# Moving ScalarE casts, batch sums and operand pieces to other work units in a fused attention and two-layer kernel

## The chip, the core and the metric

The kernel runs on one core of a Trainium2 chip. The metric is the time of one execution in microseconds (us), as the device reports it; lower is better. The engines are called as in the profile: PE is TensorE (PEld its weight loads), DVE is VectorE, ACT is ScalarE, POOL is GpSimd, SP is SyncE, which here issues nearly all DMAs.

## The reference

For 4 batches and 8 heads (sequence 768, head dimension 64) queries and keys are hashed by the signs of six projections. A score counts only where query and key fall into the same bucket; the rest get -1e9. The softmax of the scores times V is the attention output. The heads of a token side by side are a row of x, 3072 rows of 512. Then h = x @ w_in (512 x 2048), g is a piecewise function of h (0 below -1, h above 1, (h + 1)^2 / 4 between), and the result is g @ w_out (2048 x 512). All of it is float32.

## The kernel before, in words

**Split numbers.** A float32 product on PE is made of three matmuls of rounded parts: hi x hi, hi x lo, lo x hi. For every operand somebody makes the rounded part (a cast, on ACT in most places: "hi") and the rest (a subtraction, on DVE or POOL: "lo"). Much of the work beside the matmuls is of this kind, and all lo parts have the one line L39.

**Attention.** `attention` (line 125) walks over 384 units: 32 heads of 12 units, two query halves of six key tiles each. A unit, numbered head.unit from here on (16.5 is unit 5 of head 16), consists of: two score matmuls (L391, L392) into one of four score banks; two exponentials on ACT (L400 rounded, L405 exact); the rest `pl` on DVE, or for key tiles 0 and 3 on POOL; three output matmuls (L424, L426, L428) for the unit four before, in the tile order 1, 2, 0, 4, 5, 3. In the units 3 and 9 of every head ACT also copies a finished output half out of its bank (L434). Two heads ahead of use the row maxima are found: two matmuls (L323) into the only `smax` bank at the end of every even unit, and a reduction on DVE (L327) in the next. The last of them is clamped on POOL (L357, L359), turned on PE (L368) and put away.

**Tasks.** Everything else hangs on units through a list `tasks`: `at(g, fn)` runs `fn` at the end of unit g, in the order in which it was entered. An engine executes its instructions in program order, so the place of a task decides what stands behind it. The tasks that the change and the prediction speak of:

- `weights(p)`, lines 1084 to 1108, for p = 0 to 7, begins at head 3 + 3p. It loads two blocks of w_in, restores their words (ACT line L70 in unit 9, the "scaled word"; DVE L76, L79, L83 in units 9 to 2) and makes seven blocks: the hi and lo of three, the differences (`diff`, POOL), and then the hi (`shis`, ACT, L1073) and lo (`slos`, POOL) of four sums.
- Batch sums: `sums_add` (DVE L703, L704) and `sums_inv` (DVE reciprocal L708 and a DMA), lines 1127 to 1131, in head 11, 19 and 27.
- `FirstX` (line 725): operand pieces of the first batch for the second part. `load` brings data (three DMAs on SP), `fill` is one ACT instruction, `norm` two on POOL; a piece is then made by `sums` (a sum or difference of two parts), `hi` (ACT, L754) and `lo` (POOL). fx[0] and fx[1] work on 192 columns, with sums on POOL; fx[2] works on 384 columns in the heads 28 to 31, with sums on DVE (L751).
- In even heads POOL casts and splits the next q and k (`cast_h`, `low_h`, from unit 0 on), and PE uses them for the hash bits in the units 5 and 7 (L221).

**Second part.** `ffn` (line 762) walks over 224 steps k, seven to a pair of blocks of w_in (s = k % 7). Each step has six matmuls for h (L959) in one of two banks and five or six for y (L855). Step s = 0 copies its sum on ACT (`cm`, L964), and the matmuls of s = 2 go on in the same bank. Step 6 ends with two activations on ACT. `x_plan` (lines 896 to 904) makes the operand of the next batch; lines 1195 to 1209 make the hi and lo of w_out, with the cast (L96) on ACT.

Of the kernel before, what the change touches and what calls it, by code (L numbers as in the profile page):

```python
# [671 lines left out]
NBLK = 7  # L672
# [48 lines left out]
def cut(t, n):  # L721
    return t[:, n * CH:(n + 1) * CH]
# [39 lines left out]
def ffn(ctx, tc, woh, wol, xm, areas, ring, wst, wc, out, prep, post):  # L762
# [3 lines left out]
    nc = tc.nc  # L766
# [40 lines left out]
    def act_in(src):  # L807
        t = gp.tile([P, CH], F32, name="t")
        z = gp.tile([P, CH], F32, name="z", bufs=3)
        nc.scalar.activation(out=t, in_=src, func=AF.Relu, scale=0.5, bias=mh)  # L810
        nc.scalar.activation(out=z, in_=t, func=AF.Relu, scale=1.0, bias=m1)  # L811
        return [None, None, z, t]
# [81 lines left out]
    def x_plan(b, cc, raw, er, norm, made):  # L894

        at(raw, x_raw, b, cc)
        for k, n in enumerate(norm):
            after(n, x_norm, b, cc, k)
            at(er[k], x_er, b, cc, k)
        for o, n in zip((0, 1, 3, 2, 4, 5, 6), made):  # L900
            if o in SUMS:
                after(n, x_sum, o)
            after(n, x_hi, b, cc, o)
            after(n + 1, x_lo, b, cc, o)
# [8 lines left out]
    for b in range(1, B):  # L913
        n = (b - 1) * 56
        if b == 2:
            x_plan(b, 0, n + 8, range(n + 8, n + 12), [n + m for m in (15, 16, 18, 22)],
                   [n + m for m in (23, 25, 26, 28, 30, 31, 32)])
            x_plan(b, 1, n + 34, range(n + 26, n + 34, 2), [n + m for m in (37, 39, 43, 44)],
                   [n + m for m in (46, 47, 48, 50, 51, 53, 54)])
        else:  # L920
            x_plan(b, 0, n + 9, range(n + 9, n + 21, 3), [n + m for m in (16, 19, 23, 26)],
                   [n + m for m in (28, 30, 31, 32, 34, 35, 37)])
            x_plan(b, 1, n + 39, range(n + 30, n + 38, 2), [n + m for m in (43, 44, 46, 48)],
                   range(n + 49, n + 56))
    at(57, lambda: xm.sums_load(*(t[:, 0:NF] for t in pc[4:6]), B - 1))
# [17 lines left out]
    for k in range(NK):  # L943
        b, i, s = k // 56, k % 56 // NBLK, k % NBLK
        blk, o, bank = PRODUCTS[s]
# [8 lines left out]
        n = 0  # L954
# [25 lines left out]
        if src is not None:  # L980
            g = act_in(src)
# [23 lines left out]
def lsh_attn_ffn(ctx: ExitStack, tc: tile.TileContext, qk, v, pj, cv, w_in, w_out, out):  # L1005
    nc = tc.nc
# [12 lines left out]
    xm = XMaker(nc, x_d, s_d, er_d)  # L1019

    def flat(t):
        return t.rearrange("p a b s -> p (a b s)")
# [17 lines left out]
    def at(g, fn, *a):  # L1040
        tasks[g].append((fn, a))

    def conv(g, steps, offs):
        for fn, n in zip(steps, offs):
            at(g + n, fn)
# [6 lines left out]
    def wi_steps(f, dst):  # L1052
        return ws.word_steps(win_v[:, :, f * P:(f + 1) * P, :], (P, NCT, P, 2), lambda: dst, word)[1]
# [3 lines left out]
    def wo_staged(h, f):  # L1057
        stage = xdp.tile([P, DM], F32, name=f"wd{f}")
        first, *late[f] = ws.staged(wout_v[f], (P, DM, 2), stage, word)
        conv(h * NU, first, (0, 9, 10, 11, 14, 16))  # L1060
# [23 lines left out]
    def weights(p):  # L1084
        h0, r = 3 + 3 * p, rw[p % 2]
        f0, f1 = r[:, 0::3], r[:, 1:3]
        conv(h0 * NU, wi_steps(2 * p, f0), (0, 9, 10, 11, 14 - (p == 0)))
        conv((h0 + 1) * NU, wi_steps(2 * p + 1, f1), (0, 9, 10, 11, 14))
        wo_staged(h0 + 2, p)
        if p % 2 == 0:  # L1090
            his, los, subs = (26, 29), (28, 30), (32, 33, 34)
            puts, shis, slos = (34, 58), (50, 51), (52, 54)
        else:
            his, los, subs = (17, 36), (20, 40), (41, 42, 42)
            puts, shis, slos = (44, 57), (44, 45), (45, 47)
        g = h0 * NU
        for n, (d, x) in enumerate(((hp[:, 0:2], f0), (hp[:, 2:3], r[:, 2:3]))):
            at(g + his[n], hi, d, x)
            at(g + los[n], lo, d, x)
        for n, (d, x, y) in enumerate(((r[:, 0:2], r[:, 1:3], r[:, 0:2]), (r[:, 2], r[:, 2], r[:, 0]),  # L1100
                                       (r[:, 3], r[:, 2], r[:, 3]))):
            at(g + subs[n], diff, d, x, y)
        for n in range(2):
            sl = slice(2 * n, 2 * n + 2)
            at(g + shis[n], hi, hs[:, sl], r[:, sl])
            at(g + slos[n], lo, hs[:, sl], r[:, sl])
        at(g + puts[0], put, p, 0, hp)
        at(g + puts[1], put, p, 3, hs)

    for p in range(NFT // 2):  # L1110
        weights(p)
# [3 lines left out]
    g0 = (NH - 4) * NU  # L1115
# [11 lines left out]
    for b in range(B - 1):  # L1127
        g = (b + 1) * H * NU + LAG + 4
        at(g, lambda b=b: xm.sums_load(*(attn["small"].tile([P, NF], F32, name=n, bufs=1) for n in ("sm", "em")), b))
        at(g + 30, xm.sums_add)  # L1130
        at(g + 30, xm.sums_inv, b)

    def rows(t):
        return [t[:, 2 * k * CH:(2 * k + 2) * CH].bitcast(F32).rearrange("p (t n) -> p t n", t=2) for k in range(4)]

    def four(t, n):
        return [cut(t, n + k).bitcast(F32) for k in range(4)]
# [3 lines left out]
    def piece_wide(k):  # L1141
        if not wide:
# [3 lines left out]
    fx = [FirstX(nc, xm, cc, sl, pc, raw, er, lambda o, t, cc=cc: cut(wbig, 2 * NBLK * cc + 2 * o + t),  # L1146
                 lambda: attn["sv"])
          for cc, sl, pc, raw, er in ((0, slice(0, CH // 2), lambda k: xq[:, k], four(wbig, 8), rows(wbig)),
                                      (0, slice(CH // 2, CH), lambda k: xq[:, k], four(wbig, 8), rows(wbig)),
                                      (1, slice(0, CH), piece_wide, four(flat(T1[i0]), 0), rows(flat(T2[i0]))))]  # L1150
# [5 lines left out]
    def unit(h, n):  # L1156
        return h * NU + n

    def piece(x, o, g, eng_hi, eng):
        if o in FirstX.SUMS:  # L1160
            at(g, x.sums, o, eng)
        at(g + (o in FirstX.SUMS and eng_hi is not eng), x.hi, o, eng_hi)
        at(g + (eng_hi is not eng) * (1 + (o in FirstX.SUMS)), x.lo, o, eng)

    at(unit(10, 8), load_sv)
    for k, (h, n) in enumerate(((11, 6), (11, 9), (13, 6), (13, 9))):
        at(unit(h, n), fx[0].load, k)
    for n, gs in enumerate((((13, 1, 5), (13, 3, 7), (15, 1, 5), (15, 3, 10)),
                            ((23, 1, 5), (23, 3, 7), (25, 1, 4), (25, 3, 5)))):
        for k, (h, a, m) in enumerate(gs):  # L1170
            at(unit(h, a), fx[n].fill, k)
            at(unit(h, m), fx[n].norm, k)
    for n, plan in enumerate((((2, 17, 5), (0, 17, 7), (1, 17, 10), (3, 19, 3), (5, 19, 6), (4, 19, 9), (6, 21, 9)),
                              ((2, 25, 6), (0, 25, 8), (1, 25, 10), (3, 27, 9), (5, 28, 0), (4, 28, 3), (6, 28, 7)))):
        for o, h, m in plan:
            piece(fx[n], o, unit(h, m), nc.scalar, nc.gpsimd)
    for k, (n, a, m) in enumerate(((1, 9, 11), (2, 12, 13), (7, 16, 17), (9, 19, 20))):
# [2 lines left out]
        at(g0 + m, fx[2].norm, k)  # L1180
    for o, n in ((0, 22), (1, 24), (2, 26), (3, 28), (5, 31), (4, 34), (6, 37)):
        if o in FirstX.SUMS:
            at(g0 + n, fx[2].sums, o, nc.vector)
        at(g0 + n + 1, fx[2].hi, o, nc.scalar)
        at(g0 + n + 2, fx[2].lo, o, nc.gpsimd)
    for k in range(5):
# [9 lines left out]
    for f, n in sorted(starts.items(), key=lambda x: x[1]):  # L1196
        if f in late:
            get, back = late[f]
            prep[n].append((get, ()))
            n_cast, n_low = n + 3, n + 4  # L1200
        else:
            back, (s0, *steps) = ws.word_steps(wout_v[f], (P, DM, 2), ws.square)
            prep[n - 5].append((s0, ()))
            for fn, m in zip(steps, (0, 0, 1, 3)):
                post[n + m].append((fn, ()))
            n_cast, n_low = n + 4, n + 6
        cast, low = ws.split(back, woh[f], wol[f], nc.scalar, nc.vector)
        post[n_cast].append((cast, ()))
        post[n_low].append((low, ()))
    areas = [flat(t) for t in (T2[i0], T2[i1], T1[i0])], wbig  # L1210
    ffn(ctx, tc, woh, wol, xm, areas, ring, wst, wc, out, prep, post)


# [48 lines left out]
```

## Time and profile before

| what | us |
|---|---|
| median of three runs | 976.39 (975.54 to 976.45) |
| the profiled execution | 976.73 |
| its span, first to last instruction | 975.0 |
| PE busy | 955.5 (98% of the span) |
| DVE, ACT, POOL busy | 741.2, 686.8, 383.3 |

The page's slices show PE at nine tenths or more throughout, its granted clock at full speed throughout (1.00 is 2.4 GHz), and POOL at work until 465 us only: there the attention part ends. Matmuls are pipelined, and their modelled ends overlap the next start; so waits of PE are best read from starts.

### The profile page before, as it was taken

Reading aid. Unit: us, or ns where it says so; the run is one execution under the profiler, and the core shown is the slowest. Engines: PE = TensorE matmul, PEld = TensorE weight load, DVE = VectorE, ACT = ScalarE, POOL = GpSimd, SP = SyncE. Lnnn points to the kernel's source line nnn. Section 1 sums busy time; section 2 is a strip of 40 time slices with the busy share of each in tenths; the row PEclk is TensorE's granted clock in tenths of the full one; section 3 lists DMA queues with packets and bytes.
Section 4 is the critical chain, followed back from the end, with each engine's and each line's share of the span. In section 5 each row is a group of like instructions: output and inputs, shape, how many; then the busy total and the mean of one; then the engine's idle time right before and its main releaser. Section 6 shows DMA issues by size and latency. Waiting matters only on the chain.

```text
span 975.0 us, 15653 instructions
## 1 busy us (share of the span) xinstructions
PE 955.5 (98%) x5002; PEld 879.8 (90%) x5002; DVE 741.2 (76%) x1299; ACT 686.8 (70%) x1522; POOL 383.3 (39%) x512
## 2 busy tenths in 40 slices
PE   8999999999999999999999999999999999999998
PEld 7899999999899999998888898889998889888886
DVE  8778888888888888887688886677765777655554
ACT  7789999899899999999556656454564455644444
POOL 8767888778889888897000000000000000000000
PEclk9999999999999999999999999999999999999999
DMA  6775666878776677582895846765457464454431
GB/s 163 190 181 144 186 192 192 253 225 258 204 225 171 193 238 215 150 274 71 247 249 187 232 115 192 206 166 168 120 166 221 122 212 122 141 162 119 117 100 65
DMA packets 84633, 174.37 MB, mean 179 GB/s; under 512 B 13460, under 2 KB 35080, under 8 KB 83528
## 3 DMA queue, kind: packets, MB, share of 16 engines
q1 hardware_dynamic: 84282, 173.34, 61.9%
q8 instruction: 40, 0.66, 0.3%
q14 instruction: 41, 0.34, 0.1%
q10 hardware_dynamic: 270, 0.04, 0.0%
HBM read 116.35 MB, written 30.46 MB: 151 GB/s over the span
## 4 chain that ended last, share of the span: by engine, by line
PE 66%; ACT 9%; DVE 9%; DMA 5%; POOL 5%; issue 3%; SPq 1%; ACTq 0%; DVEq 0%; POOLq 0%
PE y L855 24%; PE h L959 21%; PE smax L323 4%; PE s L391 3%; PE s L392 3%; PE o L428 3%; PE o L424 3%; PE o L426 3%; ACT ph L400 2%; DVE nm L327 2%; DMA wraw<-in_w_out_dram 2%; PE o L221 2%; ACT s L405 2%; DVE pl L39 1%; POOL pl L39 1%
## 5 line engine op out<-in xcount | busy, mean ns | idle before, releaser
L400 ACT ACTIVATE ph<-s 128x384 fp32r<-128x384 f32 x380 | 190.4, 501 | 22.8 <-PE s L392 17.6
L327 DVE TENSOR_REDUCE nm<-smax 128x1 f32<-128x768 f32 x189 | 180.0, 952 | 23.1 <-PE smax L323 22.4
L39 DVE TENSOR_TENSOR pl<-s,ph 128x384 fp32r<-128x384 f32 x256 | 139.1, 551 | 34.0 <-ACT s L405 29.8
L816 DVE SCALAR_TENSOR_TENSOR t<-t 128x384 f32<-128x384 f32 x128 | 71.4, 558 | 104.4 <-ACT z L811 104.4
L39 POOL TENSOR_TENSOR pl<-pf,ph 128x384 fp32r<-128x384 f32 x128 | 130.3, 1022 | 32.4 <-ACT pf L405 32.4
L391 PE MATMUL s<-t 128*128 128x384 f32 x384 | 131.4, 342 | 1.5 <-DVE pl L39 1.5
L428 PE MATMUL o<-pl,va 128*128 128x386 f32 x384 | 130.2, 339 | 0.3 <-DVE pl L39 0.3
L424 PE MATMUL o<-ph,va 128*128 128x386 f32 x384 | 130.2, 339 | 0.2 <-DVE neg L232 0.2
L426 PE MATMUL o<-ph,vb 128*128 128x386 f32 x384 | 129.9, 338 | 0.0
L392 PE MATMUL s<-t 128*128 128x384 f32 x384 | 129.5, 337 | 0.2 <-DMA t<-te 0.2
L405 ACT ACTIVATE s<-s 128x384 f32<-128x384 f32 x252 | 127.3, 505 | 0.0
L855 PE MATMUL y<-t,ghi 128*128 128x512 f32 x384 | 125.9, 395 | 0.2 <-ACT ghi L821 0.2
L323 PE MATMUL smax<-t 128*128 128x384 f32 x378 | 101.1, 348 | 7.6 <-DVE nm L327 5.8
L821 ACT CAST ghi<-z 128x384 fp32r<-128x384 f32 x128 | 64.9, 507 | 40.9 <-DVE z L817 37.5
L959 PE MATMUL h<-wbig,t 128*128 128x384 f32 x420 | 84.5, 337 | 0.4 <-DVE cu L978 0.2
L323 PEld LDWEIGHTS smax<-t 128*128 128x128 f32 x378 | 65.3, 188 | 19.2 <-DVE nm L327 14.7
L811 ACT ACTIVATE z<-t,m 128x384 f32<-128x384 f32 x128 | 79.0, 617 | 4.2
L855 PEld LDWEIGHTS y<-t,ghi 128*128 128x128 f32 x384 | 71.5, 188 | 10.9 <-issue 0.7
L959 PEld LDWEIGHTS h<-wbig,t 128*128 128x128 f32 x420 | 75.0, 188 | 6.8 <-DVE cu L978 0.9
L391 PEld LDWEIGHTS s<-t 128*128 128x128 f32 x384 | 72.3, 188 | 4.3 <-DVE pl L39 2.3
L855 PE MATMUL y<-woh,glo 128*128 128x512 f32 x192 | 75.6, 394 | 0.2
L855 PE MATMUL y<-t,glo 128*128 128x512 f32 x192 | 75.8, 395 | 0.0
(182 smaller groups left out, 2045.5 us busy)
## 6 DMA issues: line engine op xcount, KB each, us to landing
t<-wc SPq DMA_DIRECT2D x140, 256.0 KB
t<-t SPq DMA_DIRECT2D x60, 384.0 KB
ring<-wc SPq DMA_DIRECT2D x84, 256.0 KB
raw<-in_qk_dram SPq DMA_DIRECT2D x14, 768.0 KB
wraw<-in_w_in_dram SPq DMA_DIRECT2D x16, 512.0 KB
wraw<-in_w_out_dram SPq DMA_DIRECT2D x16, 512.0 KB
wc<-wbig SPq DMA_DIRECT2D x8, 1024.0 KB
xd<-xs SPq DMA_DIRECT2D x32, 192.5 KB
```

The lines of the kernel that those rows point to most:

```text
L39: eng.tensor_tensor(out=out, in0=a, in1=b, op=ALU.subtract)
L323: nc.tensor.matmul(out=smax[hd][:, hf, 0:HS], lhsT=t2[:, 0, h, i * P:(i + 1) * P], rhs=t2[:, 1, h, hf * HS:(hf + 1) * HS], start=True, sto ...
L327: nc.vector.tensor_reduce(out=nmp(hd)[:, i:i + 1], in_=smax[hd][:, :, 0:HS], axis=AX.XY, op=ALU.max, negate=True)
L391: nc.tensor.matmul(out=ps[:, 0:HS], lhsT=t1[:, 1, h, ks], rhs=t1[:, 0, h, sl], start=True, stop=False)
L392: nc.tensor.matmul(out=ps[:, 0:HS], lhsT=t2[:, 1, h, ks], rhs=t2[:, 0, h, sl], start=False, stop=True)
L400: nc.scalar.activation(out=ph[:, 0:HS], in_=ps[:, 0:HS], func=AF.Exp, scale=SCALE)
L405: nc.scalar.activation(out=pf, in_=ps[:, 0:HS], func=AF.Exp, scale=SCALE)
L424: nc.tensor.matmul(out=o, lhsT=wa, rhs=ph, start=(jj == 0), stop=False)
L426: nc.tensor.matmul(out=o, lhsT=wb, rhs=ph, start=False, stop=False)
L428: nc.tensor.matmul(out=o, lhsT=wa, rhs=pl, start=False, stop=(jj == NJ - 1))
L855: nc.tensor.matmul(out=ys[c][m], lhsT=g_[:, m * P:(m + 1) * P], rhs=w, start=(first and k == 0), stop=(last and k == 2))
L959: nc.tensor.matmul(out=ps, lhsT=w[:, cs], rhs=x, start=(n == 0 and s not in (2, 3, 6)), stop=(n == 5), skip_group_check=True)
```

## The change

It moves tasks, and gives four sums to another engine. `shis` and `slos` get other units, `sums_inv` goes three units later than `sums_add`; loads, fills, norms and pieces of `FirstX` get other units and heads; the sums of fx[2] go from DVE to POOL; in `ffn` one piece of two batches goes a step earlier, and casts of w_out a step later.

```diff
@@ ffn, batches 1 and 3
             x_plan(b, 0, n + 9, range(n + 9, n + 21, 3), [n + m for m in (16, 19, 23, 26)],
-                   [n + m for m in (28, 30, 31, 32, 34, 35, 37)])
+                   [n + m for m in (28, 30, 31, 32, 33, 35, 37)])
@@ weights(p)
         if p % 2 == 0:
-            puts, shis, slos = (34, 58), (50, 51), (52, 54)
+            puts, shis, slos = (34, 58), (49, 51), (52, 54)
         else:
-            puts, shis, slos = (44, 57), (44, 45), (45, 47)
+            puts, shis, slos = (44, 57), (44, 47), (46, 48)
@@ batch sums
         at(g + 30, xm.sums_add)
-        at(g + 30, xm.sums_inv, b)
+        at(g + 33, xm.sums_inv, b)
@@ FirstX: loads; fill and norm (head, fill unit, norm unit); pieces (o, head, unit)
-    for k, (h, n) in enumerate(((11, 6), (11, 9), (13, 6), (13, 9))):
+    for k, (h, n) in enumerate(((11, 7), (11, 9), (12, 9), (13, 8))):
...
-    for n, gs in enumerate((((13, 1, 5), (13, 3, 7), (15, 1, 5), (15, 3, 10)),
-                            ((23, 1, 5), (23, 3, 7), (25, 1, 4), (25, 3, 5)))):
+    for n, gs in enumerate((((13, 1, 5), (13, 2, 7), (13, 7, 9), (15, 1, 6)),
+                            ((23, 1, 6), (25, 1, 4), (25, 2, 6), (25, 4, 8)))):
...
-    for n, plan in enumerate((((2, 17, 5), (0, 17, 7), (1, 17, 10), (3, 19, 3), (5, 19, 6), (4, 19, 9), (6, 21, 9)),
-                              ((2, 25, 6), (0, 25, 8), (1, 25, 10), (3, 27, 9), (5, 28, 0), (4, 28, 3), (6, 28, 7)))):
+    for n, plan in enumerate((((2, 17, 6), (0, 17, 7), (1, 17, 8), (3, 19, 3), (5, 19, 5), (4, 19, 7), (6, 21, 1)),
+                              ((2, 27, 1), (0, 27, 6), (1, 28, 0), (3, 28, 1), (5, 28, 3), (4, 28, 6), (6, 28, 9)))):
...
         if o in FirstX.SUMS:
-            at(g0 + n, fx[2].sums, o, nc.vector)
+            at(g0 + n, fx[2].sums, o, nc.gpsimd)
@@ casts of w_out in ffn
-            n_cast, n_low = n + 3, n + 4
+            n_cast, n_low = n + 3 + (n % NBLK == 3), n + 4
...
-            n_cast, n_low = n + 4, n + 6
+            n_cast, n_low = n + 5, n + 6
```

A piece with a sum takes three units: the sum in the unit given, hi in the next, lo in the one after; a piece without one takes two.

## Rows read from the trace of the kernel before

**Rows 1.** The page, engine totals: busy us, share of the span, instructions.
```profile
PE 955.5 (98%) x5002; PEld 879.8 (90%) x5002; DVE 741.2 (76%) x1299; ACT 686.8 (70%) x1522; POOL 383.3 (39%) x512
```

**Rows 2.** Busy by stretch: us, PE, PEld, DVE, ACT, POOL, clock, DMA share, GB/s.
```profile
75.00:467.00 392.00, 383.81 (x2148) 369.36 (x2147) 328.47 (x509) 360.80 (x886) 327.30 (x414) 1.00 0.69 198
480.00:960.00 480.00, 479.11 (x2376) 429.04 (x2375) 337.03 (x660) 250.86 (x472) 0.00 (x0) 1.00 0.56 162
```

**Rows 3.** Who PE waited for, 75 to 467 us: total, times, longest.
```profile
PE smax L323 <- DVE nm L327: 4.1, 12, 0.5
PE smax L323 <- DMA t<-bits: 0.6, 1, 0.6
PE s L368 <- POOL nmr L359: 0.5, 2, 0.3
```

**Rows 4.** Timeline of DVE, 175 to 178.2 us (unit 11.3): start, us, what.
```profile
176.38 0.45 DVE L708 RECIPROCAL sm<-sm 128x48 f32<-128x48 f32 x1
```

**Rows 5.** Timeline of ACT, 409.8 to 413 us (units 27.9 to 28.0).
```profile
409.96 0.49 ACT L434 COPY xs<-o 128x384 f32<-128x384 f32 x1
410.32 0.65 ACT L1073 CAST wbig<-rw 128x512 fp32r<-128x512 f32 x1
410.84 0.70 ACT L70 ACTIVATE wsq<-wraw 128x512 f32<-128x512 f32 x1
```

**Rows 6.** Timeline of DVE, 409.8 to 415.5 us.
```profile
412.40 0.56 DVE L39 TENSOR_TENSOR pl<-s,ph 128x384 fp32r<-128x384 f32 x1 [0.37 <-ACT s L405]
```

**Rows 7.** Timeline of PE, 247 to 252 us (head 16).
```profile
249.92 0.44 PE L221 MATMUL o<-t,pw 128*128 128x384 f32 x1 [0.63 <-POOL t L39]
251.86 0.23 PE L368 MATMUL s<-ident_r,nmr 128*12 128x128 f32 x1 [0.27 <-POOL nmr L359]
```

**Rows 8.** Timeline of POOL, 218 to 224.5 us (head 14).
```profile
221.98 1.02 POOL L39 TENSOR_TENSOR t<-raw,t 128x384 fp32r<-128x384 f32 x1
```

**Rows 9.** Timeline of ACT, 378 to 382.5 us (head 25).
```profile
379.27 0.35 ACT L754 CAST wbig<-xq 128x192 fp32r<-128x192 f32 x1 [0.88 <-POOL xq L747]
```

**Rows 10.** Timelines of POOL, 289 to 300 us, and of ACT, 293 to 300 us (head 19).
```profile
295.47 0.61 POOL L751 TENSOR_TENSOR xq<-xq 128x192 f32<-128x192 f32 x1
...
296.11 0.35 ACT L754 CAST wbig<-xq 128x192 fp32r<-128x192 f32 x1 [0.98 <-POOL xq L751]
```

**Rows 11.** Timeline of PE, 444 to 448.5 us (unit 30.7).
```profile
447.08 0.45 PE L391 MATMUL s<-t 128*128 128x384 f32 x1 [1.55 <-DVE pl L39]
```

**Rows 12.** Timeline of ACT, 443.5 to 451 and 451 to 464 us: the casts L754.
```profile
446.59 0.51 ACT L754 CAST wbig<-raw 128x384 fp32r<-128x384 f32 x1 [1.33 <-DVE raw L751]
449.48 0.49 ACT L754 CAST wbig<-raw 128x384 fp32r<-128x384 f32 x1
...
452.84 0.51 ACT L754 CAST wbig<-raw 128x384 fp32r<-128x384 f32 x1 [0.55 <-DVE raw L751]
455.57 0.53 ACT L754 CAST wbig<-raw 128x384 fp32r<-128x384 f32 x1
```

**Rows 13.** Timeline of POOL, 443.5 to 451 us.
```profile
444.97 1.00 POOL L39 TENSOR_TENSOR wbig<-raw,wbig 128x384 fp32r<-128x384 f32 x1
448.15 1.34 POOL L39 TENSOR_TENSOR pl<-pf,ph 128x384 fp32r<-128x384 f32 x1
449.45 0.60 POOL L96 CAST t<-wsq 128x512 fp32r<-128x512 f32 x1
450.13 1.29 POOL L39 TENSOR_TENSOR t<-wsq,t 128x512 fp32r<-128x512 f32 x1
```

**Rows 14.** The sums L751, all: duration ns min/median/max, first and last start.
```profile
L751 POOL TENSOR_TENSOR xq<-xq x8: 598/609/622, 288.1 to 421.0; 128x192 f32<-128x192 f32 x8
L751 DVE TENSOR_TENSOR raw<-raw x4: 560/1006/1410, 446.0 to 453.7; 128x384 f32<-128x384 f32 x4
```

**Rows 15.** Timelines of ACT and of PE, 540 to 544 us (steps 34 to 37).
```profile
541.13 0.60 ACT L96 CAST woh<-wsq 128x512 fp32r<-128x512 f32 x1
...
542.99 1.32 PE L959 MATMUL h<-wbig,ring 128*128 128x384 f32 x6 [0.54 <-ACT cm L964]
```

## The prediction

> **What bounds the kernel now.** I read four views. The engine totals [rows 1] show PE busy 98% of the span, ahead of DVE, ACT and POOL; so the change can only win where PE waits, and lose where it makes PE wait. The busy time by stretch [rows 2] says where that is: in the 392 us of attention from 75 on PE is idle 8.2 us, in the 480 us of the second part 0.9 us. The waits of PE by releaser [rows 3] show of what kind: twelve waits of a row-maximum matmul for DVE's reduction of the one before, 4.1 us together; single ones for a DMA and for POOL; beside them stands the longest, 1.55 us for a `pl` [rows 11]. The timelines around each wait give the burst that made it. A wait costs PE some 0.1 us more than its own length, as the next matmul starts late too; I count that in. The profiled execution took 976.73 us, 1.73 over its span and 0.34 over the median of 976.39; what I add up is taken from the profile and put on the median.
>
> **Batch sums.** In the units 11.3, 19.3 and 27.3 three small DVE instructions stand ahead of a reduction, and PE waits for it. The reciprocal of 0.45 us [rows 4] goes three units on, where DVE has gaps. Three times 0.45 us: gain 1.4.
>
> **ACT's casts of sums.** For odd p the second cast stood in unit 9, between the output copy and the scaled word. The three follow without a gap [rows 5], and DVE's `pl` then waits 0.37 us for ACT [rows 6]; two DVE steps later PE waits for the reduction. The same picture stands at 10.2, 16.2, 22.2 and 28.2. In unit 11 the cast delays only the exponentials of tile 0, whose `pl` is POOL's and not urgent. Gain 0.4 each at 10.2 and 22.2 (bounds 0 and the wait with its restart, 0.5): 0.8; 16.2 and 28.2 are counted below. For even p the edit doesn't do what it is called after: one cast leaves unit 2 for 1, the other stays in unit 3, a unit with an output copy. Nothing waits there now; I count 0.
>
> **Norms and loads.** A norm is two POOL instructions of 0.6 us. One leaves 15.5 for 13.9. In head 15 POOL runs without a gap from the clamp to the key splits of head 16, and PE waits for those splits, 0.63 us for the bits and 0.27 us for the clamp, both with a restart [rows 7]. With 1.2 us less in that queue both end; with the wait at 16.2 that is 1.1 up to the bits of 16.7, which POOL still bounds. Likewise 23.7 loses its norm; of the two waits for a clamp, 0.5 us together [rows 3], 0.23 are left for 24.6: with restart and the bits behind it I count 0.5. In head 25 ACT stands 0.88 us before a piece whose norm isn't made [rows 9], and PE then waits twice for DVE; that piece goes to 27.1. Gain 1.1, the 0.88 and two restarts.
>
> At 13.6 a load stood in SP's queue ahead of the four DMAs of the hash bits, and PE waited 0.6 us for them at 14.4 [rows 3]. The load goes to 12.9. But the norm that comes to 13.9 puts 1.2 us into POOL's queue ahead of the splits for 14.7, the last of which ended at 223.00 [rows 8], about a microsecond before PE wanted it. I take 0 for the pair, between a gain of 0.7 and a loss of 0.5.
>
> **Pieces.** In head 19 the sums stand one and two units earlier, behind the same queue. Today POOL is through with the last block rest at 295.47, and ACT's cast waits 0.98 us for the sum made then [rows 10]. After the change that sum goes ahead of the block rest, and its cast comes at some 295.0; four exponentials of 0.4 us later, at 296.9 with the cast, ACT is at the next cast, in 19.8. POOL is through with the block rest at 296.1, and has a `pl` of 1.0, a rest of 0.6 and a sum of 0.61 to do: 298.3. ACT waits 1.4 us there, and PE loses perhaps 1.2, of which it already loses 0.5 at 20.0 (one of the twelve of [rows 3]): loss 0.7 (0 to 1.2). The piece that goes from 21.9 to 21.1 meets an idle POOL: 0.
>
> Two pieces more come into head 28, where POOL and ACT have hardly a gap: four pieces of POOL's 0.6 us [rows 14], two casts of ACT's 0.3, and casts of ACT due right behind sums that POOL makes 0.7 and 0.6 us late. Loss 1.2, the gain at 28.2 included (0 to 2.3).
>
> **The last sums on POOL.** Now DVE waits at 30.6 for POOL's rest, makes the sum, and only then the `pl` that frees the score bank; PE stands 1.55 us [rows 11]. That ends. But every cast of such a piece now waits for POOL, in program order. POOL's queue, by old times: a rest from 444.97, the sum to 446.98 (1.0 each); the cast can start at 447.0, before at 446.59 [rows 12]. Behind the cast: a rest, a `pl`, the cast of w_out 0.60, and the second sum ends at 451.1; its cast began at 449.48. Then the rest of w_out 1.29 [rows 13], a rest, a `pl`, a sum: 455.5; before 452.84. Then the cast, a rest, a `pl`, the last sum: 459.1; before 455.57 [rows 12]. ACT is 3.5 us late at the fourth cast and has no gaps behind it to make that up; PE was about 0.6 behind ACT at the end. Loss 2.9, wait at 30.7 included. The lower bound is a gain of 1.7, if ACT's waits stay as they are, 1.33 and 0.55 us; the upper a loss of 3.5.
>
> In this sum POOL's `pl` takes 1.0 us, as away from DVE's sums. Beside them it took 1.34, and the sums 0.56 to 1.41 us [rows 13, 14]. The Trainium skill's page "SBUF — State Buffer", section "Who interferes with whom", says that a DVE instruction with two inputs in SBUF contends with a GpSimd instruction that reads SBUF; by that the move itself takes this away, as I assumed. Were it not so, three `pl` of 1.34 would make it 1.0 us worse.
>
> **The second part.** At step 34 the cast of w_out (0.60 us) and a piece's cast stand on ACT ahead of `cm` of step 35, and the matmuls of step 37 wait 0.54 us for that copy [rows 15]. Both move out of its way. At step 41 a cast moves likewise. PE's idle time in this part is 0.9 us in all [rows 2]; with a restart for each of two or three waits I count 1.1 (0.5 to 1.8). The other casts moved stand where PE waits for nothing: 0.
>
> **Sum.** Gains 1.4 + 0.8 + 1.1 + 0.5 + 1.1 + 1.1 = 6.0; losses 0.7 + 1.2 + 2.9 = 4.8. Net 1.2 us gained: 976.4 - 1.2 = 975.2. A measurement here tells 0.2% from no change, that is 1.95 us; so my forecast is no difference that can be told.
>
> **Rivals.** *Faster: POOL's sums hold ACT up no longer than DVE's did.* The last term turns from a loss of 2.9 into a gain of up to 1.7, so 970.6, or 972.3 if it comes to nothing. It decides from a term under about 2.1 on. For it: the 1.55 us wait is the longest of attention behind its start, and it surely goes. Against it: the queue above, in which POOL has no gap for eight microseconds.
>
> *Slower: POOL bounds from head 28 to the end of attention.* Its place is POOL's program order, its price the upper bounds of the three losses, 1.2 + 2.3 + 3.5 = 7.0, against gains of which 4.0 are kept, as in head 14 where a wait removed only brings PE sooner to POOL's next piece: 979.4. It decides when the losses outgrow the gains by 2. For it: POOL is busy 327 of 392 us already [rows 2]. Against it: it catches up once a head, before the clamp. The Trainium skill's "GPSIMD Engine Reference", section "Elementwise — side-by-side cycle accounting", speaks against the move in the same sense: there a two-input add is about twice as slow on GpSimd as on the Vector engine. The trace agrees as far as the same sum goes that DVE makes in 0.56 us alone, while POOL's operations of that size take 1.0.
>
> *Nothing but shifting:* every wait removed in attention comes back at the next burst, and the last sums cost what they free; the second part's 1.1 stays: 975.3, inside the forecast.
>
> **Chances and range.** Forecast, no difference: 0.47. Faster 0.36: the gains are single waits that I can name, while the largest loss hangs on one queue that I worked out by hand. Slower 0.17. The range takes in both rivals' nearer halves: 971.8 to 979.0.
>
> **What would show it.** Right: the reciprocal and its reduction no longer side by side, and no wait of PE behind it; no wait for DVE at 30.7; ACT's casts L754 of 384 columns waiting for POOL L751, over 4 us together; steps 37 and 44 without a wait for `cm`. Wrong: those four casts with waits under 2 us together, or the attention part ending more than 4 us earlier or at all later.

## The result, and the profile after

The change makes the kernel slower. Medians of 14 runs each: 979.36 us against 976.06 (975.54 to 977.69). One execution of the changed kernel, the one with the profile, was disturbed (1883.66 us); without it the median is 979.27 us (977.93 to 981.07), the ratio 1.0033 [1.0024, 1.0041], so 3.2 us are lost where 1.2 were forecast as a gain. In a repeat (after_again) the change was 2.4 us slower, at 978.86. The first time lies just outside the predicted range, near the 979.4 of the rival "slower"; that of the repeat lies just inside the range. The profile after is that of the repeat, which took 979.23 us with a span of 977.1; the profile before took 976.73 with a span of 975.0.

The page of the kernel after, engine totals, to set beside [rows 1]:

```profile
PE 958.1 (98%) x5002; PEld 879.2 (90%) x5002; DVE 735.9 (75%) x1295; ACT 687.2 (70%) x1522; POOL 386.5 (40%) x516
```

Busy time of the kernel after by stretch (columns as in [rows 2]):

```profile
75.00:469.00 394.00, 386.36 (x2148) 368.89 (x2148) 324.32 (x506) 361.53 (x888) 331.09 (x418) 1.00 0.69 197
482.00:962.00 480.00, 479.07 (x2377) 429.10 (x2376) 336.96 (x661) 251.06 (x472) 0.00 (x0) 1.00 0.57 163
```

Who PE waited for in the kernel after, 75 to 469 us (total, times, longest):

```profile
PE smax L323 <- DVE nm L327: 2.2, 4, 0.8
PE o L424 <- DVE ph L397: 1.6, 2, 0.8
PE s L391 <- ACT pf L405: 1.2, 3, 0.5
PE s L368 <- POOL nmr L359: 0.7, 3, 0.3
PE s L392 <- DMA t<-te: 0.7, 1, 0.7
```

Four sums went from DVE to POOL, as the counts say (1299 and 512 before, 1295 and 516 after). The waits have changed their kind. Of the twelve waits for the reduction [rows 3] four are left, 2.2 us instead of 4.1. New are two kinds that [rows 3] does not have: PE waiting for `ph`, and for ACT's exact exponential.

To see where the time went I cut the span in three by two marks that every kernel has: the first and last of the matmuls that turn the row maxima (L368, heads 2 to 30.6) and the first matmul of the second part (L959). The next two fences hold the marks of before and of after; the columns are count, duration in ns (least, median, greatest), first and last start.

```profile
L368 PE MATMUL s<-ident_r,nmr x29: 220/223/232, 57.9 to 445.3; 128*12 128x128 f32 x29
...
L959 PE MATMUL h<-wbig,t x420: 331/334/459, 465.1 to 829.7; 128*128 128x384 f32 x140
```

```profile
L368 PE MATMUL s<-ident_r,nmr x29: 220/223/232, 58.7 to 444.5; 128*12 128x128 f32 x29
...
L959 PE MATMUL h<-wbig,t x420: 331/335/443, 467.6 to 831.9; 128*128 128x384 f32 x140
```

Before: 445.3 - 57.9 = 387.4 us from head 2 to 30.6 (stretch A), 465.1 - 445.3 = 19.8 us to the second part (B), 975.0 - 465.1 = 509.9 us for the rest (C). After: 385.8, 23.1 and 509.5. So stretch A is 1.6 shorter, B (the last 17 units) 3.3 longer, C 0.4 shorter; what of A and C is the change's is worked out further down. The start before head 2 is 0.8 us longer, though the first edit stands in head 7; that is not the change's. The same cut for every kernel that ran (medians are against before on the same chip; the ratio, with its 95% interval, is not the quotient of the two medians):

| kernel | A | B | C | median us | before | ratio |
|---|---|---|---|---|---|---|
| before | 387.4 | 19.8 | 509.9 | | | |
| after_again | 385.8 | 23.1 | 509.5 | 978.86 | 976.49 | 1.0025 [1.0015, 1.0035] |
| only_sums | 387.1 | 23.0 | 509.7 | 981.00 | 976.49 | 1.0045 [1.0032, 1.0058] |
| all_but_sums | 385.2 | 19.8 | 510.3 | 975.86 | 976.49 | 0.9995 [0.9986, 1.0004] |
| only_pieces | 387.3 | 19.8 | 509.7 | 976.08 | 976.49 | 0.9997 [0.9988, 1.0005] |
| sums_casts_later | 387.3 | 19.2 | 510.0 | 975.97 | 976.52 | 0.999 [0.998, 1.0] |
| sums_no_wout | 386.8 | 21.9 | 509.7 | 978.67 | 976.52 | 1.0023 [1.0012, 1.0033] |
| only_ffn | 386.3 | 19.8 | 509.7 | 976.96 | 976.52 | 1.0003 [0.9992, 1.0013] |
| only_inv_casts | 388.2 | 19.7 | 510.2 | 977.31 | 976.52 | 1.0005 [0.9995, 1.0015] |
| dve_sums_later | 387.1 | 19.1 | 510.5 | 976.13 | 976.11 | 0.9996 [0.9987, 1.0004] |
| pieces_mended | 383.9 | 19.8 | 510.0 | 974.54 | 976.11 | 0.9989 [0.9978, 1.0] |
| ffn_casts_only | 386.9 | 19.8 | 509.6 | 976.64 | 976.11 | 1.0002 [0.9993, 1.001] |
| best | 386.4 | 19.2 | 510.8 | 973.28 | 976.11 | 0.9969 [0.9959, 0.9978] |

B is the column to trust: in the seven kernels that leave the sums and their casts as they were it reads 19.7 or 19.8 every time. A and C carry late DMA landings that differ from one execution to the next: only_ffn changes nothing in A and still reads 1.1 below before. As wholes they say something only from about a microsecond on; single waits and single heads say more.

### The profile page after: what moved, and what is told of

The parts are those of the page before. It is cut to its first block, busy times and chain, and to the rows that moved or that the text cites. A ratio compares the mean times of both kernels' runs of the same rounds, so it can differ in the third digit from the quotient of the medians.

```text
span 1881.7 us, 15643 instructions
## 1 busy us (share of the span) xinstructions
PE 1876.6 (100%) x5002; PEld 1456.6 (77%) x5002; DVE 762.9 (41%) x1295; ACT 716.8 (38%) x1522; POOL 387.6 (21%) x516
## 4 chain that ended last, share of the span: by engine, by line
PE 100%; DVE 0%; ACT 0%; issue 0%
PE y L855 29%; PE h L959 25%; PE s L391 7%; PE o L426 7%; PE o L428 7%; PE s L392 7%; PE o L424 7%; PE smax L323 7%; PE o L221 2%; PE smax L445 0%; PE s L368 0%; PE s L465 0%; PE s L240 0%; PE o L271 0%; DVE xs L249 0%; PE o L445 0%
## 5 line engine op out<-in xcount | busy, mean ns | idle before, releaser
L855 PE MATMUL y<-t,ghi 128*128 128x512 f32 x384 | 225.9, 674 | 0.0
L428 PE MATMUL o<-pl,va 128*128 128x386 f32 x384 | 215.6, 562 | 0.0
L392 PE MATMUL s<-t 128*128 128x384 f32 x384 | 214.7, 559 | 0.0
L426 PE MATMUL o<-ph,vb 128*128 128x386 f32 x384 | 214.6, 559 | 0.0
L424 PE MATMUL o<-ph,va 128*128 128x386 f32 x384 | 214.4, 558 | 0.0
L391 PE MATMUL s<-t 128*128 128x384 f32 x384 | 214.3, 558 | 0.0
L959 PE MATMUL h<-wbig,t 128*128 128x384 f32 x420 | 160.5, 558 | 0.0
L959 PEld LDWEIGHTS h<-wbig,t 128*128 128x128 f32 x420 | 124.4, 298 | 37.8 <-issue 31.5
L391 PEld LDWEIGHTS s<-t 128*128 128x128 f32 x384 | 117.5, 306 | 25.1 <-issue 18.5
L424 PEld LDWEIGHTS o<-ph,va 128*128 128x128 f32 x384 | 114.6, 298 | 21.5 <-issue 14.5
L426 PEld LDWEIGHTS o<-ph,vb 128*128 128x128 f32 x384 | 114.8, 299 | 20.1 <-issue 13.9
L855 PE MATMUL y<-wol,ghi 128*128 128x512 f32 x192 | 129.7, 675 | 0.0
L855 PE MATMUL y<-woh,ghi 128*128 128x512 f32 x192 | 129.5, 674 | 0.0
```

What stands on the lines that cost most here:

```text
L391: nc.tensor.matmul(out=ps[:, 0:HS], lhsT=t1[:, 1, h, ks], rhs=t1[:, 0, h, sl], start=True, stop=False)
L392: nc.tensor.matmul(out=ps[:, 0:HS], lhsT=t2[:, 1, h, ks], rhs=t2[:, 0, h, sl], start=False, stop=True)
L424: nc.tensor.matmul(out=o, lhsT=wa, rhs=ph, start=(jj == 0), stop=False)
L426: nc.tensor.matmul(out=o, lhsT=wb, rhs=ph, start=False, stop=False)
L428: nc.tensor.matmul(out=o, lhsT=wa, rhs=pl, start=False, stop=(jj == NJ - 1))
L855: nc.tensor.matmul(out=ys[c][m], lhsT=g_[:, m * P:(m + 1) * P], rhs=w, start=(first and k == 0), stop=(last and k == 2))
```

## The experiments

### The last sums alone, and everything but them

only_sums makes this edit to the kernel before; all_but_sums undoes it in the kernel after; after_again is the kernel after unaltered.

```diff
-            at(g0 + n, fx[2].sums, o, nc.vector)
+            at(g0 + n, fx[2].sums, o, nc.gpsimd)
```

> The changed kernel unaltered, for a profile at its usual time. Theory Q (POOL's queue in the last heads: ACT's casts wait for the sums that POOL makes): 977.5 to 980; the four casts L754 of 384 columns wait over 4 us together for POOL, against 1.9 us before for DVE, and attention ends later than before. Rival H (the sums gain; pieces in other heads lose): those casts wait under 2 us together, and PE's lost time lies in the heads 13 to 28.

> The kernel before with one edit of the change: the last four sums on POOL. Theory Q: 2.9 us slower than before (2 to 3.5), and the wait of PE for a pl at 30.7 is gone all the same. Rival H: 0.5 to 1.7 us faster, by that wait.

> The changed kernel with the last four sums back on DVE. Theory Q: about 4 us faster than before, as the gains stay and 2.9 us of loss go: 972 to 973.5. Rival H: as slow as the changed kernel or slower, 979 to 981.

Measured: only_sums is 4.5 us slower than before by medians (its profiled execution is the fastest of its five), and 3.2 by stretch B; the kernel after without this edit is 0.6 faster than before, a difference that can't be told and not the 4 us expected, and its B is back at 19.8. The edit alone costs more than the whole change. Its size between the two kernels with the rest of the change is 978.86 - 975.86 = 3.0 us, and 23.1 - 19.8 = 3.3 by the stretch.

The timeline of ACT in the kernel after, 444 to 460 us: the casts L754, which in [rows 12] wait 1.33 and 0.55 us for DVE:

```profile
446.31 0.51 ACT L754 CAST wbig<-raw 128x384 fp32r<-128x384 f32 x1 [1.82 <-POOL raw L751]
...
450.44 0.51 ACT L754 CAST wbig<-raw 128x384 fp32r<-128x384 f32 x1 [1.19 <-POOL raw L751]
...
454.57 0.51 ACT L754 CAST wbig<-raw 128x384 fp32r<-128x384 f32 x1 [1.31 <-POOL raw L751]
...
458.14 0.51 ACT L754 CAST wbig<-raw 128x384 fp32r<-128x384 f32 x1 [0.74 <-POOL raw L751]
```

5.06 us of waiting in place of 1.88. The reason stands in the timeline of POOL over the same time:

```profile
445.26 1.01 POOL L751 TENSOR_TENSOR raw<-raw 128x384 f32<-128x384 f32 x1
446.90 1.00 POOL L39 TENSOR_TENSOR wbig<-raw,wbig 128x384 fp32r<-128x384 f32 x1 [0.62 <-ACT wbig L754]
447.85 1.02 POOL L39 TENSOR_TENSOR pl<-pf,ph 128x384 fp32r<-128x384 f32 x1
448.81 0.62 POOL L96 CAST t<-wsq 128x512 fp32r<-128x512 f32 x1
449.38 1.02 POOL L751 TENSOR_TENSOR raw<-raw 128x384 f32<-128x384 f32 x1
450.36 1.29 POOL L39 TENSOR_TENSOR t<-wsq,t 128x512 fp32r<-128x512 f32 x1
```

It is a ring: the sum, then ACT's cast, for which POOL stands 0.62 us itself, then the rest of that piece, a `pl`, the cast of w_out, and only then the next sum, which the next cast on ACT waits for. PE's share of it, from the timeline of PE, 445 to 462 us:

```profile
445.07 0.44 PE L391 MATMUL s<-t 128*128 128x384 f32 x1 [0.34 <-DVE pl L39]
447.64 0.45 PE L391 MATMUL s<-t 128*128 128x384 f32 x1 [0.54 <-ACT pf L405]
451.78 0.44 PE L391 MATMUL s<-t 128*128 128x384 f32 x1 [0.36 <-ACT pf L405]
453.19 0.44 PE L424 MATMUL o<-ph,va 128*128 128x386 f32 x1 [0.79 <-DVE ph L397]
457.26 0.44 PE L428 MATMUL o<-pl,va 128*128 128x386 f32 x1 [0.36 <-DVE pl L39]
460.89 0.44 PE L424 MATMUL o<-ph,va 128*128 128x386 f32 x1 [0.80 <-DVE ph L397]
```

The one wait of 1.55 us [rows 11] has shrunk to 0.34, and five of 0.36 to 0.80 have come. None names POOL: the exponentials stand behind the casts on ACT, and PE waits for them, or for DVE's `ph` and `pl`, which are made from them.

### Which link of the ring holds ACT up

Two kernels with the sums on POOL, each opening the ring at another place: sums_casts_later puts cast and rest of the pieces with a sum two units later; sums_no_wout takes the cast and rest of w_out out of POOL's queue there. Their other edit, the sums on POOL, is that of only_sums and is left out of the cuts below.

```diff
-        at(g0 + n + 1, fx[2].hi, o, nc.scalar)
-        at(g0 + n + 2, fx[2].lo, o, nc.gpsimd)
+        at(g0 + n + (3 if o in FirstX.SUMS else 1), fx[2].hi, o, nc.scalar)
+        at(g0 + n + (4 if o in FirstX.SUMS else 2), fx[2].lo, o, nc.gpsimd)
```

```diff
-        if f == 0:
-            at(g0 + n + 5, cast)
-            at(g0 + n + 7, low)
-        else:
-            prep[0] += [(cast, ()), (low, ())]
+        prep[0] += [(cast, ()), (low, ())]
```

> The kernel before with the last four sums on POOL, and the casts and rests of those four pieces two units later, so that ACT meets each cast three units behind its sum. Theory Q (the loss is ACT standing before casts in program order): those casts wait under 1 us together, the wait of PE at 30.7 is gone too, and the heads 30 and 31 take 1 to 1.7 us less than before; in all 1 to 1.7 us faster than before. Rival K (POOL's own work makes the loss: late pl, contention with DVE): the heads 30 and 31 take 2 us or more longer than before, as with the sums alone (3.3).

> The kernel before with the last four sums on POOL, and the cast and rest of the first w_out block (1.9 us of POOL) moved from the units 30.7 and 30.9 to the start of the second part. Theory Q: 1.9 us less stands in POOL's queue ahead of the third sum and 0.6 ahead of the second, so of the 3.3 us that the heads 30 and 31 took longer 1.5 to 2 go. Rival K: POOL is as busy up to the end of attention, and 0.5 us or less goes.

The casts L754 on ACT's timeline of sums_casts_later:

```profile
446.78 0.50 ACT L754 CAST wbig<-raw 128x384 fp32r<-128x384 f32 x1
...
449.47 0.54 ACT L754 CAST wbig<-raw 128x384 fp32r<-128x384 f32 x1
...
453.26 0.51 ACT L754 CAST wbig<-raw 128x384 fp32r<-128x384 f32 x1 [0.93 <-POOL raw L751]
...
456.18 0.51 ACT L754 CAST wbig<-raw 128x384 fp32r<-128x384 f32 x1
```

and of sums_no_wout:

```profile
446.35 0.51 ACT L754 CAST wbig<-raw 128x384 fp32r<-128x384 f32 x1 [1.82 <-POOL raw L751]
...
449.92 0.51 ACT L754 CAST wbig<-raw 128x384 fp32r<-128x384 f32 x1 [0.62 <-POOL raw L751]
...
453.48 0.51 ACT L754 CAST wbig<-raw 128x384 fp32r<-128x384 f32 x1 [0.74 <-POOL raw L751]
...
457.06 0.51 ACT L754 CAST wbig<-raw 128x384 fp32r<-128x384 f32 x1 [0.74 <-POOL raw L751]
```

Two more units of distance take the waiting down to 0.93 us in all, and B from 23.0 to 19.2: the whole loss is gone with the sums still on POOL, though only 0.6 of the expected 1 to 1.7 us are gained on before. Taking w_out's 0.62 and 1.29 us out of the queue leaves 3.92 us of waiting and B at 21.9: 1.1 of the 3.2 go, less than the 1.5 to 2 expected, and the rest stays with cast and sum still one unit apart. What loses the time is not that POOL makes the sums, but that ACT, in program order, asks for them one unit later. The cast and its rest on POOL were moved together; which of the two distances matters more is not shown.

dve_sums_later is the other side of it: the sums stay on DVE, but stand with cast and rest one unit later.

```diff
         if o in FirstX.SUMS:
+            n += 1
             at(g0 + n, fx[2].sums, o, nc.vector)
```

> The kernel before with the last four sums still on DVE, each with its cast and rest one unit later. Theory Q (what costs is who stands before whom in program order): DVE no longer stands before POOL's rest with the pl of 30.4 behind it, so the wait of 1.7 us at 30.7 goes and no new one comes: the heads 30 and 31 take 1.2 to 1.8 us less, the kernel is that much faster. Rival (those two heads are bound by ACT's work, whatever the order): less than 0.5 us.

PE's timeline in it, 444 to 454 us:

```profile
445.41 0.44 PE L391 MATMUL s<-t 128*128 128x384 f32 x1 [0.33 <-DVE pl L39]
...
452.99 0.44 PE L428 MATMUL o<-pl,va 128*128 128x386 f32 x1 [0.26 <-DVE pl L39]
```

The wait of 1.55 us is down to 0.33 here too, and yet B is only 0.7 shorter, 19.1, and the median the same as before within its interval. Both kernels without the long waits end at 19.1 or 19.2. That the wait at 30.7 was worth 0.6 or 0.7 and not 1.7 in this stretch is thus shown twice, between the two forecasts. Where the rest went is seen in the starts of L391, counted from the last L368. In dve_sums_later the one behind the wait comes 1.3 us earlier than before and this holds for seven more units; then 0.5 are lost where PE waits for the `pl` at 452.99, and another 0.2 up to the end. The 0.7 that are left are mostly lost again in this profile: at the beginning of the second part ACT's cast waits for w_out's data (1.18 us, 0.62 before) and PE behind it for `ghi` (0.80 us, 0.24 before).

### The moves in attention

only_pieces has the loads, fills, norms and pieces of `FirstX` alone, only_inv_casts the casts of sums (`shis`, `slos`) and the reciprocal alone, each with its part of the change's diff, so:

```diff
 only_pieces: the loop over loads, the loop over fills and norms, the loop over pieces
 only_inv_casts:
-            puts, shis, slos = (34, 58), (50, 51), (52, 54)
+            puts, shis, slos = (34, 58), (49, 51), (52, 54)
...
-            puts, shis, slos = (44, 57), (44, 45), (45, 47)
+            puts, shis, slos = (44, 57), (44, 47), (46, 48)
...
-        at(g + 30, xm.sums_inv, b)
+        at(g + 33, xm.sums_inv, b)
```

> The kernel before with the loads, fills, norms and pieces of the first operand in their new units, and nothing else. Theory Q: gains at heads 16, 24 and 25 (2.5 us) and losses at heads 19 and 28 (1.9 us, up to 3.5) come out near nothing, 1 us faster to 1 us slower. Rival H: 2 to 4 us slower, with new waits of PE in the heads 14, 19, 20 and 28.

> The kernel before with the batch sums in two units and the casts of sums in their new units alone. What I forecast: 1.4 + 0.8 us and a part of 16.2 and 28.2, 2.5 to 3 us faster. Rival from the changed kernel's trace: the waits at 10.2 and 22.2 come back as waits for POOL's clamp at 10.6 and 22.6 (0.4 us each), so that only the batch sums' 1.4 us are left.

Neither makes a difference that can be told; for only_pieces that was expected, for only_inv_casts 2.5 to 3 us were, or 1.4 by the rival. The waits that were named do go in most places: the waits behind the reciprocal in the heads 11 and 19 are gone and that in 27 is shorter; those at 10.2, 16.2, 22.2, 28.2, 16.5 and those of head 25 are gone. That for the clamp at 16.6 is gone in only_pieces, but stands at 0.26 us in the kernel after. What came in their place, first from the timelines of only_inv_casts (PE):

```profile
166.57 0.23 PE L368 MATMUL s<-ident_r,nmr 128*12 128x128 f32 x1 [0.22 <-POOL nmr L359]
...
191.79 0.59 PE L323 MATMUL smax<-t 128*128 128x384 f32 x2 [0.55 <-DMA t<-bits]
```

then from the kernel after, the rows of PE and ACT in the timeline of all engines, heads 10, 13 and 14, and 19 and 20:

```profile
167.02 0.23 PE L368 MATMUL s<-ident_r,nmr 128*12 128x128 f32 x1 [0.21 <-POOL nmr L359]
...
211.54 0.46 ACT L741 ACTIVATE xq<-wbig,xsv 128x192 f32<-128x192 f32 x1 [0.59 <-DMA wbig<-ed]
...
215.55 0.62 PE L323 MATMUL smax<-t 128*128 128x384 f32 x2 [0.56 <-DVE nm L327]
...
297.02 0.35 ACT L754 CAST wbig<-xq 128x192 fp32r<-128x192 f32 x1 [1.44 <-POOL xq L751]
...
298.20 0.44 PE L391 MATMUL s<-t 128*128 128x384 f32 x1 [0.33 <-ACT pf L405]
...
300.15 0.62 PE L323 MATMUL smax<-t 128*128 128x384 f32 x2 [0.81 <-DVE nm L327]
```

In head 10 PE now waits 0.21 us (0.37 by its starts) for POOL's clamp four units after the wait that went; the same at 22.6 and, by its starts alone, at 26.6. The wait for the DMA of the hash bits at 191.79 stands in only_inv_casts alone, not in the kernel after with the same edits, so I take it for a late landing. In head 13 the new unit of a fill, 13.7, comes before its data: ACT stands 0.59 us for the DMA (1.07 in only_pieces), and PE waits twice at the begin of head 14 in place of the one wait for the bits that went. In head 19 the cast in 19.8 waits 1.44 us for POOL's sum, and PE loses at 20.0 to 20.2.

pieces_mended is only_pieces with these two places mended: the sums of head 19 in their old units, the third fill and norm of fx[0] in the units 13.11 and 15.0 (written as unit 24 of head 13), the fourth norm in 15.2.

```diff
-(13, 7, 9), (15, 1, 6)
+(13, 11, 24), (15, 1, 2)
...
-(5, 19, 5), (4, 19, 7)
+(5, 19, 6), (4, 19, 9)
```

> The kernel before with the new units of loads, fills, norms and pieces, but two pieces of head 19 at their old units, one fill of 13.7 at 13.11 (behind the landing of its data) and two norms before POOL's clamp of head 15. If the wait of 1.0 us at 14.0 is ACT's fill standing before its DMA, and the one of 1.5 us at 20.0 the sums standing in POOL's queue, both go back to 0.2 and to 0.4, and the kernel is 2 to 2.5 us faster than with the pieces alone in their new units. If they are owed to DMA traffic and to POOL's load as a whole, they stay.

Its waits of PE, 75 to 463 us:

```profile
PE smax L323 <- DVE nm L327: 3.5, 10, 0.5
...
PE s L391 <- DVE pl L39: 1.6, 1, 1.6
```

The two places are quiet, no wait for DVE is longer than 0.5 us but that of 30.7, and stretch A is 383.9, which is 3.4 less than only_pieces; by the starts of L368 around them the two places give 1.2 and 1.3 of it, as expected. By the ratio the kernel is 1.1 us under before, with an interval from 0 to 2.1, so that a gain is likely but not clear of nothing.

### The second part

only_ffn has the edits to `ffn` alone: casts of w_out a step later, a piece from step 34 to 33. ffn_casts_only leaves that piece at 34.

```diff
-                   [n + m for m in (28, 30, 31, 32, 34, 35, 37)])
+                   [n + m for m in (28, 30, 31, 32, 33, 35, 37)])
...
-            n_cast, n_low = n + 3, n + 4
+            n_cast, n_low = n + 3 + (n % NBLK == 3), n + 4
...
-            n_cast, n_low = n + 4, n + 6
+            n_cast, n_low = n + 5, n + 6
```

The first hunk is only_ffn's alone.

> The kernel before with the edits of the second part alone: one piece of two batches a step earlier, casts of w_out a step later. What I forecast: 1.1 us faster, no wait at the steps 37 and 44. Rival from the changed kernel's trace: nothing in sum (0.3 us faster to 0.3 slower), as a wait of y for ghi at step 35 (0.7 us) takes the place of the one at step 37.

> The kernel before with the casts of w_out a step later, but the piece of the operand where it was. If the wait of y for ghi at step 35 comes from the piece made a step earlier (ACT stands before DVE's sum with ghi behind it), it is gone here, with the wait for cm at step 37 at 0.3 us or less: 0.5 to 1 us faster. If it comes from the cast behind cm, it stays at 0.6 us and nothing is gained.

The kernel after, rows of ACT and PE in the timeline of all engines, steps 33 to 43:

```profile
541.52 0.51 ACT L889 CAST t<-pcs 128x384 fp32r<-128x384 f32 x1 [0.99 <-DVE pcs L886]
541.94 0.51 ACT L821 CAST ghi<-z 128x384 fp32r<-128x384 f32 x1
...
542.50 0.50 PE L855 MATMUL y<-woh,ghi 128*128 128x512 f32 x1 [0.49 <-ACT ghi L821]
...
559.60 1.31 PE L959 MATMUL h<-wbig,t 128*128 128x384 f32 x6 [0.43 <-DVE cu L978]
```

The wait for `cm` [rows 15] is gone, but the piece that went a step earlier asks for DVE's `pcs` too soon: ACT stands 0.99 us, `ghi` behind it is late, and the next matmul of y waits 0.49 us. The second wait, 0.43 us for `cu`, was there before, with 0.23:

```profile
556.98 1.31 PE L959 MATMUL h<-wbig,t 128*128 128x384 f32 x6 [0.23 <-DVE cu L978]
```

only_ffn alone shows the same two waits, 0.49 and 0.42. In ffn_casts_only, PE's timeline:

```profile
539.45 1.31 PE L959 MATMUL h<-wbig,t 128*128 128x384 f32 x6 [0.16 <-DVE cu L978]
...
556.45 1.31 PE L959 MATMUL h<-wbig,t 128*128 128x384 f32 x6 [0.46 <-DVE cu L978]
```

The waits for `cm` and for `ghi` are gone, a new one of 0.16 has come, and that of 0.46 stays; the 0.5 to 1 us expected were not measured. Neither kernel differs from before by more than its interval. The profiles say how little the edits are worth. From the step of matmuls that starts at 481.30 us before, which is ahead of the first edit, to the one at 961.01, the kernel after takes 479.63 us (483.57 to 963.20) where before takes 479.71: 0.1 us gained, and 0.03 and 0.04 in only_ffn and ffn_casts_only. The rest of the differences in C comes ahead of that, mostly in one wait for `ghi` behind the landing of w_out's data, which is 0.24 us before:

```profile
476.32 0.70 PE L855 MATMUL y<-t,ghi 128*128 128x512 f32 x2 [0.24 <-ACT ghi L821]
```

The kernel after, later there by 2.6 us, has no such wait; best has 1.20.

### A version that beats both

best is pieces_mended, with the reciprocal three units later and the DVE sums one unit later; the casts of sums and the second part stand as before.

```diff
 the edits of pieces_mended, and
-        at(g + 30, xm.sums_inv, b)
+        at(g + 33, xm.sums_inv, b)
...
         if o in FirstX.SUMS:
+            n += 1
```

> The mended pieces, the batch sums in two units, and the last sums on DVE one unit later, with the casts of sums and the second part as before. If the three gains add: 2.5 + 1.4 + 1.5 less what new waits take back, 3.5 to 5 us faster than before, 971.5 to 973. If every wait removed comes back at the next burst: 1 us.

973.28 us, ratio 0.9969 [0.9959, 0.9978]: 3.0 us under before by the ratio (2.8 by the medians, 3.5 to 5 were expected), where the change is 2.4 over it (after_again), so it beats both. The parts fit, without being measured one by one: 1.1 from the pieces and 0.4 from the sums by their ratios (neither told from nothing by itself), and 1.1 that its profile shows in the heads with the reciprocal (0.43, 0.43 and 0.28 between the L368 around them). Its profile is that of the longest of its ten executions, 976.32 us, and shows one reason for that length (timeline of all engines, rows of ACT and PE):

```profile
214.45 0.68 ACT L70 ACTIVATE rw<-wraw 128x512 f32<-128x512 f32 x1 [1.94 <-DMA wraw<-in_w_in_dram]
...
216.16 0.62 PE L323 MATMUL smax<-t 128*128 128x384 f32 x2 [1.54 <-DVE nm L327]
```

## Why the prediction was wrong

The prediction summed to 1.2 us gained, and 2.4 to 3.2 were lost. The step that failed is the sum of the gains: each wait removed was added as PE's for good, and for the casts of sums, head 19 and the second part what the instruction meets at its new place was left out or taken too small. The kernel after without the last sums (all_but_sums) was to gain 4.1 by the prediction's terms and gained 0.6, with an interval from 1.4 gained to 0.4 lost. The loss that the prediction put on the last sums was about right: 2.9 forecast, 3.0 between these two kernels.

Which gains failed is read head by head, from one L368 to the next (unit 6 of each head), in the profiles before and after:

| heads | before us | after us | difference (+ is lost) | forecast | moved there |
|---|---|---|---|---|---|
| 9 to 10 | 15.24 | 15.40 | +0.16 | -0.4 | cast of sums |
| 21 to 22 | 15.30 | 15.38 | +0.08 | -0.4 | cast of sums |
| 10 to 11 | 12.97 | 12.68 | -0.29 | -0.45 | reciprocal |
| 18 to 19 | 12.97 | 12.52 | -0.45 | -0.45 | reciprocal |
| 26 to 27 | 13.08 | 12.82 | -0.26 | -0.45 | reciprocal |
| 15 to 16 | 16.55 | 15.42 | -1.13 | -1.1 | norm, cast of sums |
| 23 to 24 | 15.20 | 14.71 | -0.49 | -0.5 | norm |
| 24 to 26 | 28.98 | 27.91 | -1.07 | -1.1 | fills, norms, a piece |
| 19 to 20 | 15.47 | 16.81 | +1.34 | +0.7 | two sums |
| 27 to 29 | 26.92 | 27.74 | +0.82 | +1.2 | two pieces more, cast of sums |

all_but_sums has the same differences within 0.03 us, and four kernels without an edit ahead of head 30 (only_ffn, only_sums, sums_no_wout, dve_sums_later) read within 0.05 of before in every row. Other spans are not so firm: from head 11 to 12, where no edit acts, these four are 0.4 to 0.8 shorter than before, and the kernel after is 0.5 shorter; from 13 to 14 they are up to 0.5 shorter, and the kernel after is 0.2 longer.

- **Last sums on POOL, 2.9 lost: right in mechanism, a little small.** By the prediction's starts ACT's waits are some 1.7, 1.2, 1.6 and 0.9 us; they are 1.82, 1.19, 1.31 and 0.74. PE lost 3.3. Of the marks named, over 4 us of waits for POOL L751 came (5.06), and no long wait stood at 30.7; but so did a mark of being wrong, as attention ends later, with the second part starting at 467.6 us instead of 465.1. What I had not seen is that the gain inside it is 0.6, not 1.7 (sums_casts_later, dve_sums_later), so the lower bound of a gain of 1.7 was out of reach, and with it most of the rival "faster".
- **`pl` at 1.0 instead of 1.34 us: right.** In the kernel after it takes 1.02 us in the row at 447.85, where [rows 13] has 1.34 at 448.15 beside a sum of DVE. The Trainium skill's rule ("SBUF — State Buffer", section "Who interferes with whom") that I leaned on agrees with the trace here. So does that of "GPSIMD Engine Reference", section "Elementwise — side-by-side cycle accounting", about twice as slow on GpSimd: 1.02 us for a sum on POOL against 0.56 for the shortest on DVE [rows 14].
- **Batch sums, 1.4 gained: right, a little large.** Two of three waits are gone and the third is shorter; 1.0 us came in the kernel after, 1.2 in only_inv_casts.
- **Casts of sums, 0.8 gained: wrong.** The waits are gone, but nothing is gained: 0.2 are lost in the two heads, 0.5 in only_inv_casts, as PE waits at POOL's clamp in unit 6 of the same heads. That clamp was in [rows 3] and in the text, as the thing that bounds the end of a head; I counted it for the norms and not here.
- **Norms, and the piece of head 25, 1.1 + 0.5 + 1.1 gained: right.** 2.7 came, so not every removed wait comes back, though the clamp's wait at 16.6, which was to end, stays. The pair at head 14, put at 0, is not told from nothing; but in it the new fill stands before its DMA, which I had not looked at, since I followed the load's DMAs only into the queue they left.
- **Head 19, 0.7 lost: right in mechanism, undersized.** ACT's wait was forecast at 1.4 us and is 1.44; PE lost 1.3, more than the upper bound of 1.2. **Head 28, 1.2 lost:** 0.8; 28.2 goes, and at 29.0 PE waits 0.68 us for the DMA of `te`, 0.18 before.
- **Second part, 1.1 gained: wrong.** 0.1 came. I moved the piece's cast out of the way of `cm` and didn't ask whether its operand was there a step earlier. It wasn't, by 0.99 us, and `ghi` of the same step stood behind it.

By these figures 3.8 us were gained and 5.7 lost. The sum is 3 us off the forecast: the casts 1.0, the second part 1.0, head 19 0.6, the batch sums and the last sums 0.4 each, and head 28 0.4 the other way. The rival "slower" names the ground, that PE then meets the next piece of the same queue, but its 979.4 is near the measured time by luck: it kept 4.0 us of the gains, close to the 3.8 that came, but set 7.0 us of loss against them.

What stays open: the figures above make some 1.9 us lost, the medians 2.4 and 3.2. About 0.3 of the gap lies outside the span, from first to last instruction, and is no matter of chance: the executions of the kernel after take 1.78 to 2.15 us more than their span, those of before 1.65 to 1.78. Why is not shown. The pair of profiles also differs by 0.8 us ahead of head 2. The runs of only_sums say more than their profile too, 4.5 against 3.2. The DMA landings that differ from run to run may hold the rest, but one profile for each kernel can't show that.

## What to carry to other kernels

When an instruction moves in a program-ordered queue, ask two questions at its new place: is its operand there by then, and who stands behind it. A sum given to a slower engine cost nothing here with its reader three units behind it, and 3 us with its reader in the next unit. Before adding up a removed wait, look for the next thing that the waiting engine needs: here 2.7 us of waits for POOL's norms were gained in full, while those behind the casts came back four units later. And compare single heads, from one mark to the next, before whole spans: they agreed within 0.05 us where the spans differed by 1.

## What the runs showed of the hardware

The longer `pl` on POOL is tied to the overlap itself and not to the place. In dve_sums_later, POOL's timeline reads 1.30 us for the `pl` at 445.68, beside DVE's sum of 445.56 to 446.12, and 1.02 for the next at 450.07, beside none. On DVE's side the same sum takes between 0.56 and 1.41 us [rows 14]; on POOL, with no sum on DVE, all four take 1.00 to 1.03. In the overlaps of before it is the instruction that starts second that takes longer: DVE's sum of 447.41, begun during POOL's rest of 447.18 (1.02 us, as alone), takes 1.21, and POOL's `pl` of 448.15, begun during that sum, takes 1.34. The other sums of these two profiles, with the POOL instructions beside them, go the same way.

What differs from one execution to the next in these profiles is when DMAs land: for the load of w_in that ACT meets late in head 13 it waited 1.94 us in the profile of best and 0.32 in that of pieces_mended, whose order of work is the same there. That this makes most of the spread is a reading of a few profiles, not more.
